# Attention on one core: scores by rows, P turned by DMA and V as the stationary operand in every second unit

## The chip, the cores and the metric

The kernel runs on one core of a Trainium2 chip. The metric is the device time in microseconds (us). All runs used here are in the fast state, except one single run (turn4) whose state is unknown; executions of one kernel mostly agree within 0.3%. PE is TensorE's matmul row in the traces and PEld its weight loads; ACT is ScalarE, DVE VectorE, POOL GpSimd, and SP is SyncE, whose queue issues the transposes. The *landing* of a transfer is the time from its issue until all its data has arrived. A ratio is the mean time of one kernel's runs over that of the other's of the same rounds, so it is not quite the ratio of the medians that are quoted.

## The reference, cut to what matters

```python
h = _layernorm(x) * (1 + ca) + sa                      # x: 2048 x 512
q = h @ wq                                             # 32 query heads of 128
k, v = repeat(k_cache, 4), repeat(v_cache, 4)          # 8 key/value heads, 2048 keys
scores = q @ k.T * 128 ** (-0.5)
p = softmax(scores)
o = p @ v
x = x + ga * (o @ wo)                                  # 4096 -> 512
# ... then a gated MLP with a 2048 x 2048 spatial matmul
```

## The kernel before

A *unit* is one of the 8 key/value heads with one tile of 128 queries: four query heads, 512 (head, query) columns, 2048 keys. There are 128 units. The loop runs one iteration per unit, in eight slots. In each slot PE computes the scores of unit `it` and the product P times V of the unit before.

Scores are computed *by columns*: keys on the partitions, (head, query) along the columns. The exponential writes P in just that layout, which P times V needs: contraction over keys, so keys on partitions. P is the stationary operand (the weight), and a column of ones beside V gives the sums of the softmax for nothing but one column.

```python
def qk(u, i):                       # slot i of unit u
    s_ps = bank2()                  # one of two score buffers, 128 x 1024
    for h in range(2):
        kt = 2 * i + h
        nc.tensor.matmul(s_ps[:, h * 512 : (h + 1) * 512],
                         lhsT=kT[:, kt * P : (kt + 1) * P],
                         rhs=qTs[b][:, :, jj * P : (jj + 1) * P])
    nc.scalar.activation(out=pTs[u][:, 2 * i : 2 * i + 2, :], in_=s_ps, func=ACT.Exp, ...)

def pv(u, i):                       # 64 matmuls of 129 columns per unit
    ...
        nc.tensor.matmul(o_ps[:, hh % 2, 0 : DH + 1],
                         lhsT=pTs[u][:, kt, hh * P : (hh + 1) * P],   # P: the weight
                         rhs=v1[:, kt, 0 : DH + 1])                   # V and the ones
    ...                             # reciprocal of the sums, multiplication, then:
    nc.sync.dma_start_transpose(out=oTs[u], in_=onorms[u])            # 128 KB

for it in range(NU + 6):
    for i in range(8):
        qk(it, i); pv(it - 1, i)
        ...                         # query projection (slots 0-3), output projection (4-7)
```

Cuts are marked by dots; tile shapes and flags are left out.

## Time and profile before

| | before |
|---|---|
| time, median (range) of the three runs before the prediction | 1321.16 us (1320.73 to 1321.49) |
| PE busy, and share of the chain | 99%, 99% |
| weight loads (PEld) | 65% of the span, beside the matmuls |
| ACT, DVE busy | 82%, 36% |
| transposing and plain DMA issued by SP (queue 1) | 37.65 MB |

"Busy" says little of PE, whose matmuls overlap. The column to read is the last one of a group, the idle time before it, and beside it the spacing from start to start. The lines are in the prediction.

### The profile page before, as it was taken

To read this page: it belongs to the slowest core of one execution; us is meant where nothing else is said; L and a number is where in the kernel's file an instruction comes from. 1 tells how busy PE (TensorE), PEld (TensorE's weight loads), DVE (VectorE), ACT (ScalarE), POOL (GpSimd) and SP (SyncE) were. 2 spreads that over 40 slices of the span, in tenths; PEclk is the share of its full clock that TensorE was granted. 3 is DMA by queue.
4 is the path that set the end of the run, shared out by engine and by line. 5 is a ranking of instruction groups with operands and counts; after the bars stand their busy time and mean duration, and the time that the engine had idled before them with its cause. 6 is when DMAs were issued, how large, how long until landed. Compare 5 with 4: busy or idle time off the path is not lost.

```text
span 1319.7 us, 27930 instructions
## 1 busy us (share of the span) xinstructions
PE 1312.4 (99%) x12359; PEld 858.6 (65%) x12359; DVE 470.7 (36%) x1162; ACT 1077.1 (82%) x1061; POOL 51.4 (4%) x96
## 2 busy tenths in 40 slices
PE   9999999999999999999999999999999999999998
PEld 5666666666666666666666666666666666644445
DVE  5622222222222222222222222222222566794444
ACT  7899999999999999999999999999999999650000
POOL 1201000000000000000000000000000000020000
PEclk9999999999999999999999999999999999999999
DMA  6542121112101111211110211121111112144300
GB/s 180 146 99 46 21 45 37 37 17 50 37 17 37 30 37 37 33 33 38 33 38 13 53 38 33 17 53 22 33 13 21 25 31 32 34 114 81 70 20 26
DMA packets 148944, 58.64 MB, mean 44 GB/s; under 512 B 138480, under 2 KB 144880, under 8 KB 148816
## 3 DMA queue, kind: packets, MB, share of 16 engines
q1 hardware_dynamic: 141792, 37.65, 15.4%
q0 software_dynamic: 4432, 16.91, 4.5%
q10 hardware_dynamic: 2592, 2.23, 0.5%
q8 instruction: 98, 1.61, 0.5%
q14 instruction: 30, 0.25, 0.1%
HBM read 21.89 MB, written 2.10 MB: 18 GB/s over the span
## 4 chain that ended last, share of the span: by engine, by line
PE 99%; DVE 0%; ACT 0%; issue 0%; DVEq 0%
PE o_ps L995 35%; PE s_ps L973 33%; PE misc L1027 8%; PE misc L940 8%; PE misc L1336 7%; PE s_ps L1182 2%; PE s_ps L1221 2%; PE o_ps L1357 1%; PE o_ps L781 1%; PE s_ps L1357 1%; PE misc L850 0%; DVE hT L809 0%; PE misc L1344 0%; ACT pT L980 0%; DVE tmp L1369 0%; DVE yout L1370 0%
## 5 line engine op out<-in xcount | busy, mean ns | idle before, releaser
L980 ACT ACTIVATE pT<-s_ps 128x1024 bf16<-128x1024 f32 x1024 | 1043.8, 1024 | 82.0 <-PE s_ps L973 6.7
L995 PEld LDWEIGHTS <-pT 128*128 128x128 bf16 x8192 | 548.5, 98 | 241.2
L995 PE MATMUL o_ps<-v,pT 128*128 128x129 bf16 x8192 | 631.5, 220 | 0.0
L973 PE MATMUL s_ps<-qT,kT 128*128 128x512 bf16 x2048 | 608.9, 379 | 0.3 <-ACT pT L980 0.2
L1006 DVE RECIPROCAL rall<-o_ps 128x2 f32<-128x2 f32 x256 | 43.5, 170 | 744.5 <-PE o_ps L995 741.1
L973 PEld LDWEIGHTS <-kT 128*128 128x128 bf16 x2048 | 199.3, 98 | 119.2 <-issue 0.8
L1027 PE MATMUL misc<-wo_g,oT 128*128 128x512 bf16 x512 | 194.1, 379 | 0.0
L940 PE MATMUL misc<-hT,wq_g 128*128 128x512 bf16 (+2 forms) x528 | 190.7, 371 | 0.1
L1007 DVE TENSOR_TENSOR onorm<-o_ps,rall 128x256 bf16<-128x256 f32 x256 | 108.6, 424 | 8.8
L1336 PE MATMUL misc<-wsp,z 128*128 128x512 bf16 (+2 forms) x560 | 100.7, 336 | 0.0
L951 DVE CAST qT<-misc 128x512 bf16<-128x512 f32 x127 | 86.2, 679 | 2.0 <-PE misc L940 2.0
L1336 PEld LDWEIGHTS <-z 128*128 128x128 bf16 x560 | 50.6, 98 | 48.5
L1040 DVE TENSOR_TENSOR xacc<-misc,xacc 128x512 f32<-128x512 f32 x112 | 76.0, 678 | 0.0
L940 PEld LDWEIGHTS <-wq_g 128*128 128x128 bf16 x528 | 50.4, 98 | 1.2 <-issue 0.4
L1027 PEld LDWEIGHTS <-oT 128*128 128x128 bf16 x512 | 50.1, 98 | 0.8
L1351 DVE TENSOR_TENSOR gb<-misc,bsp_bc 128x512 bf16<-128x512 f32 (+1 forms) x28 | 18.4, 658 | 58.9 <-PE misc L1336 58.9
L1182 PE MATMUL s_ps<-win_sb,hT 128*128 128x448 bf16 x128 | 27.0, 352 | 0.0
L1192 ACT ACTIVATE z<-s_ps 128x896 bf16<-128x896 f32 x16 | 14.7, 917 | 14.9 <-PE s_ps L1182 14.9
L1221 PE MATMUL s_ps<-hT,win_sb 128*128 128x512 bf16 x112 | 24.5, 379 | 0.0
L1229 ACT ACTIVATE z1T<-s_ps 128x1024 bf16<-128x1024 f32 x14 | 14.3, 1023 | 10.1 <-PE s_ps L1221 9.1
L692 DVE BATCH_NORM_STATS2 bnst<-x_sb 128x6 f32<-128x512 bf16 x32 | 21.8, 683 | 1.3 <-DMA x_sb<-in_A_x_dram 0.8
L1357 PE MATMUL o_ps<-wout_sb,yT 128*128 128x512 bf16 x84 | 20.1, 379 | 0.0
(88 smaller groups left out, 269.6 us busy)
## 6 DMA issues: line engine op xcount, KB each, us to landing
wq_g<-in_A_wq_dram POOLq DMA_DIRECT2D x7, 512.0 KB, 3.8
v<-in_A_v_cache_dram POOLq DMA_DIRECT2D x7, 512.0 KB, 6.0
wo_g<-in_A_wo_dram POOLq DMA_DIRECT2D x7, 512.0 KB, 4.7
oT<-onorm SPq DMA_TRANSPOSE x128, 2.4
wsp<-in_w_mod_dram POOLq DMA_DIRECT2D x1, 2048.0 KB, 9.0
out_dram<-yout ACTq DMA_DIRECT2D x16, 128.0 KB, 1.7
win_sb<-in_B_w_in_dram POOLq DMA_DIRECT2D x1, 1792.0 KB, 7.8
x_sb<-in_A_x_dram SPq DMA_DIRECT2D x3, 512.0 KB, 5.6
```

What stands on the lines that cost most here:

```text
L940: nc.tensor.matmul(ps[0][:, o0 : o0 + n], lhsT=wqs[g][:, dt, hh * DH : (hh + 1) * DH], rhs=hTs[ch][:, dt, c0 : c0 + n], start=(dt == 0), s ...
L951: nc.vector.tensor_copy(out=dst, in_=src)
L973: nc.tensor.matmul(s_ps[:, h * 512 : (h + 1) * 512].rearrange("p (r q) -> p r q", r=REP), lhsT=groups[g]["kT"][:, kt * P : (kt + 1) * P], ...
L980: nc.scalar.activation(out=pTs[u][:, 2 * i : 2 * i + 2, :], in_=s_ps[:].rearrange("p (k q) -> p k q", k=2), func=ACT.Exp, scale=inv_sqrt_dh,)
L995: nc.tensor.matmul(o_ps[:, hh % 2, 0 : DH + 1], lhsT=pTs[u][:, kt, hh * P : (hh + 1) * P], rhs=groups[g]["v1"][:, kt, 0 : DH + 1], start=( ...
L1007: nc.vector.tensor_tensor(out=onorms[u][:, hh - 1 : hh + 1, :], in0=o_ps[:, :, 0:DH], in1=rall[:, c0 : c0 + 2].unsqueeze(2).to_broadcast([ ...
L1027: nc.tensor.matmul(X_ps[:], lhsT=oTs[u][:, hh, :], rhs=groups[g]["wo"][:, hh, :], start=(hh == 0), stop=(hh == REP - 1),)
L1040: nc.vector.tensor_tensor(out=xaccs[j][:], in0=X_ps[:], in1=xaccs[j][:], op=ALU.add)
L1182: nc.tensor.matmul(ps[0][:, hf * 512 : hf * 512 + FC], lhsT=h2Ts[j // CT][:, dt, (j % CT) * P : (j % CT + 1) * P], rhs=win_sb[:, dt, FH + ...
L1221: nc.tensor.matmul(ps[0][:, k * 512 : (k + 1) * 512], lhsT=win_sb[:, dt, f * P : (f + 1) * P], rhs=h2Ts[2 * ch2 + k][:, dt, :], start=(dt ...
L1336: nc.tensor.matmul(g_ps[:, :n], lhsT=z2[:, st, f * P : (f + 1) * P], rhs=wsp[t][:, st, c0 : c0 + n], start=(st == 0), stop=(st == NT - 1 a ...
L1357: nc.tensor.matmul(dst, lhsT=yT[:, f, jj * P : (jj + 1) * P], rhs=wout_sb[:, f, :], start=(f == 0), stop=(f == NFT - 1),)
```

## The change

Its apparent intent is to cut the number of P times V matmuls and weight loads by four. With V as the weight, one load serves all four heads, and 512 columns of P stream past it: 16 matmuls of 512 columns in place of 64 of 129. The ones column is gone then (V fills all 128 weight columns), so the sums must come from elsewhere. In the changed units the scores are computed *by rows* (queries on partitions), where ACT can sum along the row while it exponentiates. But then P lies the wrong way round, and DMA has to turn it: four transposes of 512 KB per unit. Every second unit does it (even units 12 to 110, 50 in all; all units would probably be too much, since with half of them the DMA engines are already busy 73 to 89% in mid-attention, but no run tried it), and its P times V runs three iterations later instead of one.

```diff
+    TURN_A, TURN_B = 3 * CT, (HKV - 1) * NT            # 12, 112
+    def by_rows(u):
+        return TURN_A <= u < TURN_B and u % 2 == 0
+    def pv_at(u):
+        return u + 3 if by_rows(u) else u + 1
@@ qk
+        if by_rows(u):
+            hh, half = divmod(i, 2)
+            for c in range(2):
+                ...  matmul(s_ps[...], lhsT=qTs[b][:, hh, ...], rhs=kT[:, k0 : k0 + 512])
+            nc.scalar.activation(out=pn[hh][...], in_=s_ps[:], func=ACT.Exp,
+                                 scale=inv_sqrt_dh, accum_out=rsums[u][:, i : i + 1])
+            if half == 1:
+                at(*divmod(u * NSLOT + i + 2, NSLOT), lambda: turn_rows(u, hh))
+    def turn_rows(u, hh):            # sums added, reciprocal, P scaled in place, then
+        ...
+        nc.sync.dma_start_transpose(out=pTs[u][:, :, hh * P : (hh + 1) * P], in_=pn[hh])
+    def pv_rows(u, i, n):
+        for kt in range(i * NKT // n, (i + 1) * NKT // n):
+            nc.tensor.matmul(o_pss[u][:], lhsT=groups[g]["v1"][:, kt, 0:DH],
+                             rhs=pTs[u][:, kt, :], ...)
+        if i == n - 1:
+            nc.vector.tensor_copy(out=oTs[u][:], in_=o_pss[u][:]...)
@@ buffers and loads
+    pn = three slices of win_sb and one of wmod_a      # free at that time
+    odd units keep P in the buffer "wsp"
+    win_sb and the first spatial weights are loaded after unit 114
+    query projection of block 4 moves to iteration 13, which has no P times V
```

(Iteration 113 gets two P times V products.)

More of the change, by code (lines that the diff above doesn't have):

```diff
@@ L655 @@
     mhalf = res.tile([P, CT], FP32, name="mhalf")
-    win_sb = res.tile([P, NDT, F], BF16, name="win_sb")
+    win_t = res.tile([P, NDT * F], BF16, name="win_sb")
+    win_sb = win_t[:].rearrange("p (k f) -> p k f", k=NDT)
     wmod_a = res.tile([P, NDT, 2 * D], BF16, name="wmod_a")
+    pn = [win_t[:, r * SK : (r + 1) * SK] for r in range(REP - 1)]
+    pn.append(wmod_a[:].rearrange("p k n -> p (k n)")[:, 0:SK])
     wmod_b = wspp.tile([P, NDT * 4 * D], BF16, name="wsp")[:].rearrange(
@@ L926, with qproj @@
     warm(2)
-    def qproj(b, heads, c0, n):
+    def qproj(b, heads, c0, n, banks=("misc", "misc")):
         g, ch = divmod(b, NCH)
@@ L937, in mm @@
             if dt == 0 and (not one or hh == heads[0]):
-                ps[0] = bank("misc")
+                ps[0] = bank(banks[hh % 2])
             o0 = (hh - heads[0]) * n if one else 0
@@ L958 @@
     NU = HKV * NT
-    pTs, onorms, oTs, xaccs, o_pss, h2Ts = {}, {}, {}, {}, {}, {}
+    TURN_A, TURN_B = 3 * CT, (HKV - 1) * NT
[3 more added lines that the diff above has]
+        return u + 3 if by_rows(u) else u + 1
+    rsums, pTs, onorms, oTs, xaccs, o_pss, h2Ts = {}, {}, {}, {}, {}, {}, {}
     later = {}
@@ L968, in qk @@
         if i == 0:
-            pTs[u] = late.tile([P, NKT, 512], BF16, name="pT")
-        s_ps = bank2()
+            if TURN_A <= u <= TURN_B + 1 and u % 2 == 1:
+                pTs[u] = wspp.tile([P, NT, 512], BF16, name="wsp")
+            else:
+                pTs[u] = late.tile([P, NKT, 512], BF16, name="pT")
+            if by_rows(u):
+                rsums[u] = stat.tile([P, NSLOT], FP32, name="rs")
+        s_ps = bank2()
+        if by_rows(u):
+            hh, half = divmod(i, 2)
+            for c in range(2):
+                k0 = (2 * half + c) * 512
+                nc.tensor.matmul(
+                    s_ps[:, c * 512 : (c + 1) * 512],
+                    lhsT=qTs[b][:, hh, jj * P : (jj + 1) * P],
+                    rhs=groups[g]["kT"][:, k0 : k0 + 512],
+                    start=True,
+                    stop=True,
+                )
+            nc.scalar.activation(
+                out=pn[hh][:, half * HK : (half + 1) * HK],
+                in_=s_ps[:],
+                func=ACT.Exp,
+                scale=inv_sqrt_dh,
+                accum_out=rsums[u][:, i : i + 1],
+            )
+            if half == 1:
+                at(*divmod(u * NSLOT + i + 2, NSLOT), lambda: turn_rows(u, hh))
+            return
         for h in range(2):
@@ L985, in qk @@
         )
+    def turn_rows(u, hh):
+        c0 = u * REP + hh
+        rs, rinv = rsums[u], rall[:, c0 : c0 + 1]
+        tot = stat.tile([P, 1], FP32, name="tot")
+        nc.vector.tensor_tensor(
+            out=tot[:], in0=rs[:, 2 * hh : 2 * hh + 1], in1=rs[:, 2 * hh + 1 : 2 * hh + 2], op=ALU.add
+        )
+        nc.vector.reciprocal(out=rinv, in_=tot[:])
+        nc.vector.tensor_scalar(
+            out=pn[hh], in0=pn[hh], scalar1=rinv, scalar2=None, op0=ALU.mult
+        )
+        nc.sync.dma_start_transpose(
+            out=pTs[u][:, :, hh * P : (hh + 1) * P], in_=pn[hh]
+        )
+    def pv_rows(u, i, n):
+        g = u // NT
+        if i == 0:
+            o_pss[u] = bank("o_ps")
+        for kt in range(i * NKT // n, (i + 1) * NKT // n):
+            nc.tensor.matmul(
+                o_pss[u][:],
+                lhsT=groups[g]["v1"][:, kt, 0:DH],
+                rhs=pTs[u][:, kt, :],
+                start=(kt == 0),
+                stop=(kt == NKT - 1),
+            )
+        if i == n - 1:
+            oTs[u] = late.tile([P, REP, P], BF16, name="oT", bufs=3)
+            nc.vector.tensor_copy(
+                out=oTs[u][:], in_=o_pss[u][:].rearrange("p (r q) -> p r q", r=REP)
+            )
     def pv(u, i):
@@ L1144 @@
     at(2, 5, lambda: nc.gpsimd.dma_start(out=wmod_b, in_=wmod_dram[:, :, 2 * D : NMOD]))
-    at(5, 5, lambda: nc.gpsimd.dma_start(out=win_sb[:], in_=win_dram))
+    at(TURN_B + 3, 5, lambda: nc.gpsimd.dma_start(out=win_sb, in_=win_dram))
     at(9, 4, mod_cols_b)
@@ L1149, in set_fill @@
     def set_fill(b):
-        fs = qproj(b, list(range(REP)), 0, 512)
+        hole = TURN_A + 1 if (TURN_A + 1) // CT == b - 1 else None
+        fs = qproj(b, list(range(REP)), 0, 512, ("misc", "o_ps" if hole else "misc"))
         for k, fn in enumerate(fs):
             it, slot = (b - 1) * CT + k // NDT, k % NDT
+            if hole:
+                it, slot = hole, k // 2
             if b == 1:
@@ L1161, in wsp0 @@
         wsp[0] = wspp.tile([P, NT, 512], BF16, name="wsp")
-    at(20, 0, wsp0)
+    at(TURN_B + 4, 0, wsp0)
     for st in range(NT):
-        at(21 + 6 * st, 2, lambda st=st: load_wsp(wsp[0], 0, st))
+        at(TURN_B + 4 + st // 2, 2 + 4 * (st % 2), lambda st=st: load_wsp(wsp[0], 0, st))
     for g in range(1, HKV):
@@ L1257, with pv_part @@
         at(NU + 5, 5 + ch, lambda ch=ch: z2_norm(ch))
+    def pv_part(u, i, n):
+        if by_rows(u):
+            return pv_rows(u, i, n)
+        for k in range(NSLOT // n):
+            pv(u, i * (NSLOT // n) + k)
     for it in range(NU + 6):
@@ L1266 @@
             zs["z2"] = z2p.tile([P, NT, FH], BF16, name="z2")
-        wf = wo_proj(it - 3) if 3 <= it < NU + 3 else []
+        pvs = [u for u in (it - 3, it - 1) if 0 <= u < NU and pv_at(u) == it]
+        wos = [u for u in (it - 5, it - 3) if 0 <= u < NU and pv_at(u) + 2 == it]
+        wf = [fn for u in wos for fn in wo_proj(u)]
         for i in range(NSLOT):
@@ L1272 @@
                 qk(it, i)
-            if 1 <= it <= NU:
-                pv(it - 1, i)
+            if len(pvs) == 1:
+                pv_part(pvs[0], i, NSLOT)
+            elif pvs:
+                n = NSLOT // 2
+                pv_part(pvs[i // n], i % n, n)
             for fn in fill.pop((it, i), []):
                 fn()
-            if i >= 4 and wf:
-                wf[i - 4]()
+            if i >= NSLOT - len(wf):
+                wf[i - NSLOT + len(wf)]()
             if it >= NU:
                 zrun(3)
-        if 3 <= it < NU + 3 and it - 3 >= (HKV - 1) * NT:
-            ln2(it, (it - 3) % NT)
+        for u in wos:
+            if u >= (HKV - 1) * NT:
+                ln2(it, u % NT)
         if it == NU + 2:
```

## The prediction

> **What bounds the kernel now.** I read the page first (busy shares, the chain that ended last), then the costliest groups, then the order of time inside one slot of the attention loop, then ACT where it runs without waiting, then the DMA issues.
>
> ```profile
> span 1319.7 us, 27930 instructions
> ...
> PE 1312.4 (99%) x12359; PEld 858.6 (65%) x12359; DVE 470.7 (36%) x1162; ACT 1077.1 (82%) x1061; POOL 51.4 (4%) x96
> ...
> PE 99%; DVE 0%; ACT 0%; issue 0%; DVEq 0%
> ...
> L980 ACT ACTIVATE pT<-s_ps 128x1024 bf16<-128x1024 f32 x1024 | 1043.8, 1024 | 82.0 <-PE s_ps L973 6.7
> ...
> L995 PE MATMUL o_ps<-v,pT 128*128 128x129 bf16 x8192 | 631.5, 220 | 0.0
> L973 PE MATMUL s_ps<-qT,kT 128*128 128x512 bf16 x2048 | 608.9, 379 | 0.3 <-ACT pT L980 0.2
> L1006 DVE RECIPROCAL rall<-o_ps 128x2 f32<-128x2 f32 x256 | 43.5, 170 | 744.5 <-PE o_ps L995 741.1
> ```
>
> The chain is PE from end to end, and neither the scores (L973) nor P times V (L995) ever waits: 0.3 and 0.0 us of idle time before them. So time is the sum of PE's start-to-start spacings. A mean duration (220, 379 ns) is not the spacing, because matmuls overlap; the order of time gives it:
>
> ```profile
> 480.93 0.59 PE L973 MATMUL s_ps<-qT,kT 128*128 128x512 bf16 x2
> 481.36 0.62 PE L995 MATMUL o_ps<-v,pT 128*128 128x129 bf16 x8
> 481.82 0.38 PE L940 MATMUL misc<-hT,wq_g 128*128 128x512 bf16 x1
> 482.03 0.59 PE L973 MATMUL s_ps<-qT,kT 128*128 128x512 bf16 x2
> ```
>
> This is one slot, 1.10 us: two score matmuls of 512 columns, eight P times V matmuls of 129, one other of 512. From the starts in the trace between 250 and 1000 us, a matmul of 512 columns takes 215.85 ns to the next start and one of 129 columns 56.65 ns. A unit is eight slots: 16 x 215.85 + 64 x 56.65 + 8 x 215.85 = 3.45 + 3.63 + 1.73 = 8.81 us, which is the spacing of the turned-output transfers in the DMA queue (1.24 + 7.57).
>
> ACT does one exponential of 1024 columns per slot. Where PE has run ahead it goes back to back:
>
> ```profile
> 1128.69 4.69 ACT L980 ACTIVATE pT<-s_ps 128x1024 bf16<-128x1024 f32 x5
> ```
>
> The first four start-to-start spacings here are 0.90 us (4.69 less the last duration of 1.06, over four, within 10 ns). So ACT can do a slot in 0.90 and is paced by PE at 1.10: 0.20 us per slot in hand, and no more.
>
> **What the Trainium skill says.** "TensorE: Matmul & The Clock Gate", section "Back-to-back issue gap", gives about 81 ns per matmul of 128 columns in a stream of load-and-multiply pairs, and 56 ns for the bare gap. This trace has 56.65 ns with a new weight load for every one of them, so here the loads (98 ns each, beside the matmuls) cost nothing and the smaller figure holds. That decides what the change can win. "ScalarE: Activation LUTs", section "What ACT_TABLE_LOAD costs": an ACTIVATE with immediate scale takes 186 ns + 0.833 ns per column, and consecutive ones overlap by about 93 ns. For 1024 columns that is 1039 and a spacing of 946; the trace has 1.02 and 0.90, close and a little better. I found no page that prices ACT's sum output; "VectorE: DVE Perf Modes", section "Two Vector instructions with no wait between them", says that on Vector an op with accumulator output is two instructions. "DMA: Bandwidth & Descriptors", section "Latency and other measured facts", has 261 GB/s for a transposing DMA with a broken-up middle dimension; the trace has less:
>
> ```profile
> 498.26 1.83 SPq L739 DMA_TRANSPOSE kT<-in_A_k_cache_dram  x1
> ...
> 532.25 1.19 SPq L1015 DMA_TRANSPOSE oT<-onorm  x1
> ```
>
> The first moves 512 KB and is done with its packets about 2.6 us after the first of them, the second 128 KB in 0.66 us: both near 200 GB/s. The queue is held 1.83 us for the large one (1.36 in other groups) and 1.19 us for the small one.
>
> **The change, part by part.** By rows are the even units from 12 to 110: 50 units.
>
> *PE.* Scores: the same 16 matmuls of 512 columns, operands swapped. P times V: 64 matmuls of 129 columns (3.626 us) become 16 of 512 (3.454 us). That is 64 x 129 = 8256 columns against 8192, and 48 fewer starts at roughly 2.5 to 3 ns (56.65 ns less 129/2.4). Gain 0.172 us per unit, x 50 = 8.6 us. The 48 weight loads that go were hidden already. The two shapes alternate: P times V of a row unit runs three iterations later, beside the scores of an odd unit, so each iteration has still one P times V.
>
> *The hole.* Iteration 13 has no P times V and iteration 113 has two. Query projections are moved into 13, which leaves 12, 14 and 15 thin. PE sums: 12 and 14: 20 x 0.2158 + 3.63 = 7.94 us each; 13: 36 x 0.2158 = 7.77; 15: 32 x 0.2158 = 6.91; together 30.6. ACT in the same four: two column units at 8 x 0.90 = 7.2 and two row units at 8.4 to 9.2, together 31.2 to 32.8. PE idles here for about 1.5 us, once.
>
> *ACT.* Same 1024 columns per call, plus reading out the sum, in 8 x 50 = 400 calls. With the page's fixed 186 ns and overlap of 93, a one-column extra instruction adds between 0.09 (overlapped) and 0.19 (alone): an estimate of 1.0 to 1.1 us per call against a slot of 1.10. If it is more, ACT falls behind inside a row unit, but there are two score buffers: score matmuls i+2 must start 1.77 us after scores i end (two slots less 0.43), and the exponential needs 1.02 plus a hand-over of say 0.07, so ACT may lag by about 0.68 us before PE stops. The next unit pays it back at (1.08 - 0.90) x 8 = 1.4 us. So PE sees nothing until 8 x (call - 1.10) exceeds 0.68, a call of 1.19 us.
>
> *DVE.* Removed per row unit: two reciprocals (170 ns) and two multiplications (424), 1.2 us. Added: four times an add and a reciprocal (about 170 each) and a scaling of 2048 columns. Scalings with two pointers took 306, 404 and 504 ns at 128, 512 and 896 columns, 0.26 ns per column, so some 0.8 us; with the copy of the output (679, as the other 512-column copies) 5.2 us. Per pair of units DVE goes from 5.1 to 9.1 us of 17.4. All off the chain: each PSUM bank that it frees has four slots of time.
>
> *DMA.* One 128 KB transpose per row unit goes, four of 512 KB come: at 200 GB/s 2.6 us each, 10.5 us per pair, 11.2 with the one left, of 17.4 us, or 64% of the engines. The last is issued one slot into the next unit and read at the start of the third: about 14 us for an issue of 1.4 to 1.8 and 2.6 of transfer. The other loads (projection weight, moved spatial weights) keep to stages with room.
>
> Sum: 1321.2 - 8.6 + 1.5 = 1314 us.
>
> **Rivals.**
> 1. *ACT becomes the bound in row units.* For it: only 0.20 us in hand per call, and nothing in this trace shows what the sum costs. Against: the lag allowance. A call of 1.23 us means 8 x 0.13 - 0.68 = 0.36 us of stall per row unit, 18 us in all, 1332 us. A call of 1.27 gives 0.68 x 50 = 34: 1348. I give 25% to any visible stall and about 8% to one beyond 1.27.
> 2. *The DMA queue's issue time.* If issuing grew with bytes from the small SBUF transposes (4 x 1.19 = 4.8 us), four plus one small are 20.3 us in a pair of 17.4: +2.9 x 50, about 1459 us. For it: both the small one and the new ones read SBUF, the cheap large one reads DRAM. Against: the 512 KB one held the queue 1.36 to 1.83 us only. 6%.
> 3. *Fewer weight loads free PE.* If the 98 ns loads cost PE something, 48 fewer per unit would win more. Against: 56.65 ns is shorter than one load, so they overlap wholly. 2%.
> 4. *All is hidden and nothing is won.* The transposes share SBUF with PE's reads, or small waits at the iteration borders eat 8.6 us: 1318 to 1323.
>
> **Range and chances.** The certain part of the gain is 0.65%, so faster by over 2% needs rival 3. The low end allows full gain, no hole and a little from the removed waits: 1306. The high end is rival 1 at a call of about 1.24: 1338. Slower by over 2% (over 1347.6) is the far part of rival 1 and rival 2: 13%.
>
> **What would show it.** Page of the changed kernel: PE still 99% of the chain; P times V split into 4992 matmuls of 129 columns and 800 of 512; the latter spaced 215.8 ns; row-unit iterations 8.81 us and odd ones 8.63. ACT's exponentials with sum spaced no more than 1.10 us when they pair with a row unit; idle time before L973's successors near 0 outside iterations 12 to 15. The new transposes hold the queue under 2 us and land within 5; DMA share some 60 to 70% in the middle; DVE about 44% busy. Wrong if the score matmuls of row units wait on ACT (rival 1), if the V-weighted matmuls wait on the transposes or the DMA queue never idles (rival 2), or if the iterations are not shorter although nothing waits (rival 4).

## The result, and the profile after

The changed kernel takes 1316.16 us (1315.49 to 1317.03, 4 runs) against 1321.06 us, ratio 0.9963 (95% interval 0.9946 to 0.9980): the same at 2%, faster by 0.37%. The prediction had 1314.0.

The page of the changed kernel, with the lines that answer to those of before; a group's columns are line, engine, operation, output and inputs, shapes and count, then busy time and mean ns of one, then the idle time before them and what ended it:

```profile
span 1314.1 us, 25092 instructions
...
PE 1305.1 (99%) x9959; PEld 755.5 (57%) x9959; DVE 657.4 (50%) x1612; ACT 1105.0 (84%) x1461; POOL 52.0 (4%) x96
...
PE 98%; DMA 1%; DVE 0%; issue 0%; ACT 0%; ACTq 0%; DVEq 0%
...
L1013 PE MATMUL s_ps<-qT,kT 128*128 128x512 bf16 x1248 | 370.9, 379 | 1.9 <-ACT wmod_a L1001 1.6
L1001 ACT ACTIVATE win_sb<-s_ps 128x1024 bf16<-128x1024 f32 x300 | 307.0, 1025 | 6.2 <-ACT win_sb L1001 0.8
...
L1069 PE MATMUL o_ps<-v,wsp 128*128 128x129 bf16 x3264 | 251.6, 220 | 0.0
L994 PE MATMUL s_ps<-kT,qT 128*128 128x512 bf16 x800 | 237.9, 379 | 0.0
L1048 PE MATMUL o_ps<-pT,v 128*128 128x512 bf16 x800 | 237.3, 379 | 0.0
...
L1035 DVE TENSOR_SCALAR win_sb<-win_sb,rall 128x2048 bf16<-128x2048 bf16 x150 | 113.0, 753 | 5.7 <-DVE rall L1034 0.5
...
L1001 ACT ACTIVATE wmod_a<-s_ps 128x1024 bf16<-128x1024 f32 x100 | 102.4, 1024 | 2.3 <-DMA pT<-wmod_a 2.3
```

There are 2400 fewer matmuls, and PE is the chain as before. The row scores (L994) and both kinds of P times V (L1048, L1069) wait for nothing. New is a small idle time before the column scores (L1013, 1.9 us where there were 0.3), ended by ACT; and in the last line ACT itself waits 2.3 us for a transposing DMA. The chain has 1% of DMA for the same reason.

One slot of an odd iteration, in which the P times V of a row unit runs (order of time, PE; start us, duration):

```profile
489.25 0.59 PE L1013 MATMUL s_ps<-qT,kT 128*128 128x512 bf16 x2
489.68 0.59 PE L1048 MATMUL o_ps<-pT,v 128*128 128x512 bf16 x2
490.11 0.38 PE L944 MATMUL misc<-hT,wq_g 128*128 128x512 bf16 x1
490.32 0.38 PE L1013 MATMUL s_ps<-qT,kT 128*128 128x512 bf16 x1
```

Slot to slot it is 1.07 to 1.08 us, where the kernel before had 1.10. Over a pair of iterations, from one output copy of a row unit to the next, the median is 17.44 us; two units of before take 2 x 8.81 = 17.62.

Busy time in a stretch of 150 us in mid-attention, before and then after. The columns are PE, weight loads, DVE, ACT and GpSimd in us (with counts), the granted clock, the DMA engines' share and GB/s:

```profile
850.00:1000.00 150.00, 150.00 (x1501) 101.74 (x1500) 40.48 (x102) 139.45 (x137) 2.13 (x3) 1.00 0.15 29
```

```profile
850.00:1000.00 150.00, 150.00 (x1115) 85.59 (x1114) 70.22 (x174) 145.42 (x202) 2.87 (x4) 1.00 0.73 144
```

Everything but PE has more to do: DVE 70 us for 40, the DMA engines 73% for 15%. PE is still full, and only the 0.17 us per row unit come out at the end.

**Where the time went.** For every matmul I took the time to the next start and subtracted the steady spacing of its shape; what remains is PE not working at its pace. The sums, in us:

| stretch | before | after |
|---|---|---|
| start to 110 us | 6.84 | 6.58 |
| 110 to 150 us (iterations 12 to 15) | 0.00 | 1.13 |
| 150 to 1000 us | 0.06 | 1.77 |
| 1000 to 1140 us (two products in one iteration) | 0.23 | 0.55 |
| 1140 us to the end | 1.78 | 1.78 |
| total | 8.92 | 11.80 |

The shape gives 50 x 0.172 = 8.6 us, and 2.9 are lost again: -5.7 us, against spans of 1319.7 and 1314.1 (-5.6). The 1.77 us of the third stretch are one single stop, at 541 us. ACT in order of time there, with the idle time and what ended it in brackets:

```profile
539.88 0.19 ACT L1001 ACTIVATION_READ_ACCUMULATOR win_sb<-s_ps 128x1 f32 x1
542.18 1.02 ACT L1001 ACTIVATE wmod_a<-s_ps 128x1024 bf16<-128x1024 f32 x1 [2.11 <-DMA pT<-wmod_a]
```

ACT may not overwrite the fourth head's rows (`wmod_a`) until the transpose of the unit before has read them. That one, from the DMA queue of SP, and what GpSimd issued then:

```profile
528.82 2.60 SPq L1038 DMA_TRANSPOSE pT<-wmod_a  x1
```

```profile
528.90 0.75 POOL L720 DMA_DIRECT2D wq_g<-in_A_wq_dram  x1 [64.68 <-PE misc L944]
```

A 512 KB weight load went out on GpSimd's own queue 0.08 us after the transpose. The transpose landed after 13.3 us (the median of all is 4.6), the load after 12.2 (3.8 in the kernel before). In mid-attention ACT comes back to the fourth head's buffer 11.0 us (median) after its transpose was issued; PE reads the turned rows only after 13.0. The load waits for the last query projection of an earlier group, which ends in slot 3 of an odd iteration, just where the fourth head's transpose starts: the schedule brings the two together in every group of 16 units.

### The profile page after: what moved, and what is told of

It reads as the page before. It is cut to its first block, busy times and chain, and to the rows that moved or that the text cites. A ratio compares the mean times of both kernels' runs of the same rounds, so it can differ in the third digit from the quotient of the medians.

```text
span 1314.1 us, 25092 instructions
## 1 busy us (share of the span) xinstructions
PE 1305.1 (99%) x9959; PEld 755.5 (57%) x9959; DVE 657.4 (50%) x1612; ACT 1105.0 (84%) x1461; POOL 52.0 (4%) x96
## 4 chain that ended last, share of the span: by engine, by line
PE 98%; DMA 1%; DVE 0%; issue 0%; ACT 0%; ACTq 0%; DVEq 0%
PE o_ps L1069 21%; PE s_ps L1013 20%; PE o_ps L1048 13%; PE s_ps L994 13%; PE misc L1101 8%; PE misc L944 8%; PE misc L1426 7%; PE s_ps L1260 2%; PE s_ps L1299 2%; PE o_ps L1447 1%; DMA pT<-wmod_a 1%; PE o_ps L785 1%; PE s_ps L1447 1%; PE misc L854 0%; PE o_ps L944 0%; DVE hT L813 0%
## 5 line engine op out<-in xcount | busy, mean ns | idle before, releaser
L1020 ACT ACTIVATE wsp<-s_ps 128x1024 bf16<-128x1024 f32 x408 | 416.2, 1025 | 19.5 <-PE s_ps L1013 3.5
L1013 PE MATMUL s_ps<-qT,kT 128*128 128x512 bf16 x1248 | 370.9, 379 | 1.9 <-ACT wmod_a L1001 1.6
L1001 ACT ACTIVATE win_sb<-s_ps 128x1024 bf16<-128x1024 f32 x300 | 307.0, 1025 | 6.2 <-ACT win_sb L1001 0.8
L1069 PEld LDWEIGHTS <-wsp 128*128 128x128 bf16 x3264 | 218.5, 98 | 96.3
L1069 PE MATMUL o_ps<-v,wsp 128*128 128x129 bf16 x3264 | 251.6, 220 | 0.0
L994 PE MATMUL s_ps<-kT,qT 128*128 128x512 bf16 x800 | 237.9, 379 | 0.0
L1048 PE MATMUL o_ps<-pT,v 128*128 128x512 bf16 x800 | 237.3, 379 | 0.0
L1020 ACT ACTIVATE pT<-s_ps 128x1024 bf16<-128x1024 f32 x216 | 217.3, 1026 | 20.6 <-PE s_ps L1013 8.3
L1013 PEld LDWEIGHTS <-kT 128*128 128x128 bf16 x1248 | 121.0, 98 | 117.0 <-issue 4.4
L1069 PEld LDWEIGHTS <-pT 128*128 128x128 bf16 x1728 | 115.3, 98 | 49.6
L1048 PEld LDWEIGHTS <-v 128*128 128x128 bf16 x800 | 78.2, 98 | 94.4
L1069 PE MATMUL o_ps<-v,pT 128*128 128x129 bf16 x1728 | 132.5, 220 | 0.0
L994 PEld LDWEIGHTS <-qT 128*128 128x128 bf16 x800 | 78.2, 98 | 52.5 <-issue 0.2
L1001 ACT ACTIVATE wmod_a<-s_ps 128x1024 bf16<-128x1024 f32 x100 | 102.4, 1024 | 2.3 <-DMA pT<-wmod_a 2.3
```

Of the source, the lines that this page charges most:

```text
L994: nc.tensor.matmul(s_ps[:, c * 512 : (c + 1) * 512], lhsT=qTs[b][:, hh, jj * P : (jj + 1) * P], rhs=groups[g]["kT"][:, k0 : k0 + 512], sta ...
L1001: nc.scalar.activation(out=pn[hh][:, half * HK : (half + 1) * HK], in_=s_ps[:], func=ACT.Exp, scale=inv_sqrt_dh, accum_out=rsums[u][:, i : ...
L1013: nc.tensor.matmul(s_ps[:, h * 512 : (h + 1) * 512].rearrange("p (r q) -> p r q", r=REP), lhsT=groups[g]["kT"][:, kt * P : (kt + 1) * P], ...
L1048: nc.tensor.matmul(o_pss[u][:], lhsT=groups[g]["v1"][:, kt, 0:DH], rhs=pTs[u][:, kt, :], start=(kt == 0), stop=(kt == NKT - 1),)
L1069: nc.tensor.matmul(o_ps[:, hh % 2, 0 : DH + 1], lhsT=pTs[u][:, kt, hh * P : (hh + 1) * P], rhs=groups[g]["v1"][:, kt, 0 : DH + 1], start=( ...
```

## The experiments

**Theory.** The gain is the shape of P times V on PE alone, 0.172 us per row unit, mostly fewer starts (a start here is one matmul with its weight load, beyond its columns). Sums, scaling and turning are hidden; what was lost is the hole at iteration 12 and the stop behind the weight load. **Rivals.** (a) The sums on ACT cost time in every row unit. (b) The gain is the dropped ones column, not the starts. (c) The transposes cost PE time without a visible wait. (d) The stop is nearly full DMA engines, not the meeting of two queues. Twelve kernels were run; all passed the comparison with the reference, those with a constant for the sums too, since here all of P is near 1/2048. The traces of vw50, vw_all, rows54, turn4 and the four kernels with extra ACT work lack a few per cent of the matmul records, so for those I read pair lengths and not gaps.

### after_again: the changed kernel once more

No edit.

> The changed kernel unaltered, as the yardstick of this series. Both theories: 1316 us. What it tells beside that: whether the one stop of PE of 1.8 us at 541 us in the first profile (score matmuls behind ACT, ACT behind the transposing DMA of the fourth head that was issued in the same tenth of a microsecond as a 512 KB weight load) comes back in another execution. If it belongs to the schedule it stands at the same place; if it is chance it is gone or elsewhere, and the runs of one kernel spread by some 1.5 us.

Measured: 1315.01 us (1314.64 to 1319.15, 5 runs), ratio 0.9963. Its profiled execution (1314.64 us) has no stop: 0.0 us of lost PE time between 150 and 1000 us, and 10.52 us in all. Without the stop the kernel is within 0.7 us of the predicted 1314.0. So whether PE stops in a given execution is chance, at a place that the schedule offers again and again; over nine executions the kernel spreads by 4.5 us, the kernel before by 0.8.

### wq_sync: the weight loads behind the transposes in one queue

```diff
-        at(it + 7, 3, lambda g=g: load_wq(g, nc.gpsimd))
+        at(it + 7, 3, lambda g=g: load_wq(g, nc.sync))
```

> Only the weight loads of the query projection move from GpSimd's queue to the SP queue, behind the fourth head's transpose. If the stop of 1.8 us comes from those loads running on a second queue beside the transposes, it goes and the time falls by 1 to 2 us to about 1314.5, with no PE gap over 0.5 us between 160 and 1000 us. If the stop is only the DMA engines being nearly full, the same bytes on one queue keep it: 1316.

Measured: 1314.28 us (1313.80 to 1314.30, 5 runs), ratio 0.9946. The stop is gone (0.0 us lost between 150 and 1000 us), and the spread falls from 4.5 to 0.5 us. The 95% intervals of the two ratios overlap, so the spread and the traces carry this, not the means. The SP queue in order of time:

```profile
215.16 2.03 SPq L1038 DMA_TRANSPOSE pT<-wmod_a  x1
217.25 0.94 SPq L720 DMA_DIRECT2D wq_g<-in_A_wq_dram  x1
218.24 3.70 SPq L743 DMA_TRANSPOSE kT<-in_A_k_cache_dram  x1
```

Rival (d) falls: in the 14 us after such a transpose the DMA engines move 179 to 206 GB/s at a busy share of 0.93 to 1.04 (four places), which is no idle stretch (113 GB/s at 1.17 around the stop, 528 to 542 us), and still no turned head after 130 us whose landing is recorded takes over 7 us.

But the edit changes two things at once. The load shares the queue, and it is issued 1.8 to 2.1 us behind the transpose, some 12 iterations later than on GpSimd's queue, which issued it as soon as its buffer was free. Which of the two helps, the one queue or the distance, is not separated.

The other profiles of this series support that the meeting matters: in v64 and in nosum, which keep GpSimd's loads, PE stopped for 1.6 and 1.4 us, each time behind a fourth head's transpose issued within 0.2 us of such a load and landing after 13.2 and 13.0 us. The four traces have 20 meetings of a load with a fourth head's transpose within 0.8 us. In the six where the transpose was issued 0.03 to 0.2 us before the load, it landed after 8.7 to 13.3 us; in the other 14 (later than the load, or more than 0.3 us before it) after 5.7 to 7.7. Three of the six stopped PE. So two queues alone do not make a transpose late; it goes by tenths of a microsecond, which differ from execution to execution; what the engines do in that case, the traces do not tell. That the slow unprofiled executions (1319.15 us) had more than one stop is likely and not shown.

### v64: V as the weight, but loaded again for each head

```diff
-        for kt in range(i * NKT // n, (i + 1) * NKT // n):
-            matmul(o_pss[u][:], lhsT=v1[:, kt, 0:DH], rhs=pTs[u][:, kt, :])
+        for m in range(i * REP * NKT // n, (i + 1) * REP * NKT // n):
+            hh, kt = divmod(m, NKT)
+            matmul(o_pss[u][:, hh * P : (hh + 1) * P], lhsT=v1[:, kt, 0:DH],
+                   rhs=pTs[u][:, kt, hh * P : (hh + 1) * P])
```

> V stays the weight, but each weight load is repeated for every head: 64 matmuls of 128 columns per row unit instead of 16 of 512; everything else is as in the changed kernel. Theory (the gain is 48 fewer starts at about 3 ns and 64 fewer columns): 64 x 56.3 = 3.60 us against 3.45, so +0.149 us x 50 = +7.5 us, about 1323.5, slower than the kernel before. Rival (the gain is the 64 columns of sums alone, 0.027 us per unit, and starts are free): +0 us, 1316.

Measured: 1322.08 us (1320.09 to 1324.93), ratio 1.0013: 7.1 us above the changed kernel, and the gain is gone. The pair takes 17.56 us against 17.44. So 48 starts cost 0.12 us, 2.5 ns each; that makes 55.8 ns for a matmul of 128 columns, not the 56.3 of the expectation, and 50 x 0.12 = 6 us of the 7.1; the stop in its profile is part of the rest. Rival (b) falls: of the 0.172 us per unit, 0.12 are starts and 0.05 are left for the ones column. v64 has all the weight loads back, and their 98 ns stay hidden. From its page between 250 and 1000 us:

```profile
L1049 PE MATMUL o_ps<-pT,v 128*128 128x128 bf16 x2725 | 207.8, 219 | 0.0
L1049 PEld LDWEIGHTS <-v 128*128 128x128 bf16 x2722 | 180.6, 98 | 80.2
```

But every matmul here has a load of its own, so v64 adds 48 loads and 48 matmuls together. Whether the 2.5 ns belong to the start of the matmul or to the change of weight, no run separates.

### nosum: ACT does not sum

```diff
                 scale=inv_sqrt_dh,
-                accum_out=rsums[u][:, i : i + 1],
@@
-                rsums[u] = stat.tile([P, NSLOT], FP32, name="rs")
+                rsums[u] = rs_const          # filled with 1024.0 once
```

> ACT no longer sums in the row units; a constant stands for the sums (results only near the reference, since all P are close to 1/2048). 400 reads of 0.19 us leave ACT, 78 us of its time. Theory (they fit in the slot, ACT is not on the chain outside the four thin iterations): row-unit exponentials go back to where PE paces them, time falls by 0.5 to 1.2 us, all of it between 117 and 150 us: 1315. Rival (the sums cost time in every row unit): falls by 4 us or more.

Measured: 1315.65 us (1314.27 to 1318.09), ratio 0.9959: no different from the changed kernel (1315.01). Unit 12, in the thin iterations, takes 7.94 us instead of 8.21; the pairs stay at 17.44. Rival (a) falls. The expected saving of about 1 us cannot be told from the scatter of the stops.

### vw50: V as the weight alone

```diff
# on the kernel before, in the same 50 units
+        if v_weights(u):
+            for kt in (2 * i, 2 * i + 1):
+                matmul(o_pss[u][:], lhsT=v1[:, kt, 0:DH], rhs=pTs[u][:, kt, :])
+            # last slot: oT = o_ps * (1 / 2048), instead of the sums
```

> One part alone, on the kernel before: in the same 50 units V is the weight of P times V, but scores stay by columns, P is not turned, ACT sums nothing, and the output is scaled by a constant 1/2048 in place of the sums (results only near the reference). No hole, no large transposes. Theory: -0.172 us x 50 = -8.6 us, and -0.0 elsewhere: 1312.5. The difference to the changed kernel, about 3.5 us, is then the price of the rest (hole, end, the one stop). Rival (the turned transposes take bandwidth from PE or the swapped score operands cost something): well under 1312.

Measured: 1313.02 us (1312.30 to 1313.17), ratio 0.9936: -8.15 us, where 8.6 were expected. The pair is 17.44 us, the same as with all the turning and summing. Rival (c) falls with it: 144 GB/s of DMA traffic, mostly transposes, do not change PE's spacing. The price of the rest is 1314.28 - 1313.02 = 1.3 us with the repaired load, and 2 to 3 us without.

### vw_all: the same in 116 units

```diff
# on vw50
-        return 3 * CT <= u < (HKV - 1) * NT and u % 2 == 0
+        return u >= 3 * CT
```

> V as the weight in every unit from 12 on (116 units), scores by columns, a constant in place of the sums, nothing turned: what the shape alone is worth. Theory: 116 x 0.172 = 20.0 us less than 1321.1, about 1301, if DVE and ACT stay off the chain (ACT 0.90 against a slot of 1.08). Rival (at a slot of 1.08 ACT, or the weight loads of V, begin to hold PE): less than 2.3 times the gain of the 50 units.

Measured: 1302.25 us (1301.84 to 1303.28), ratio 0.9859: -19.0 us, 2.3 times the gain of the 50 units, and the unit is 8.633 us long. The shape is worth the same in every unit. (By the core's span, 1299.7 us at the median against 1319.4, it is 19.7 us, close to the 20.0 reckoned; the rest lies outside the span.) But this kernel has no true sums, so it is a bound and not a version.

### act_half and act_full: more work on ACT in row units

```diff
                 accum_out=rsums[u][:, i : i + 1],
             )
+            if i % 2 == 1:                   # act_half; act_full: always
+                nc.scalar.activation(out=idle[:, 0:8], in_=ident[:, 0:8], func=ACT.Exp, ...)
```

> The changed kernel with an idle 8-column exponential after every second summed exponential: 200 more instructions on ACT. Theory (ACT may lag 0.68 us in a row unit before PE stops, and the next unit pays it back): four extra operations of 0.1 to 0.2 us are 0.4 to 0.8 us of lag, so 0 to 0.1 us per unit: 1316 to 1322. Rival (ACT at 1.10 us per call is already the pace of row units): +0.4 to 0.8 us x 50, 1336 to 1356.

> The same after every summed exponential: 400 more instructions. Theory: eight extra operations of 0.1 to 0.2 us are 0.8 to 1.6 us of lag less the allowance of 0.68: 0.1 to 0.9 us x 50 = 5 to 46 us, 1322 to 1362, and score matmuls of the row units wait on ACT. From both runs together the allowance can be read: stall per unit should be 8 x extra - 0.68 here and 4 x extra - 0.68 (or nothing) in the other. Rival: twice the loss of the other run.

Measured: 1318.08 us (1317.59 to 1318.30) and 1317.88 us (1316.12 to 1319.39), both ratio 0.9976. The pair is 17.44 us in both. The cost is the 2 to 3 us that the first turned units lose (unit 14 takes 11.8 and 10.9 us in place of 8.3 to 9.1; ACT waits there up to 2.4 us for transposes). It turned out that these runs could not test the lag allowance. Where ACT is limited, in unit 12 of after_again, the order of time shows

```profile
118.86 1.02 ACT L1001 ACTIVATE win_sb<-s_ps 128x1024 bf16<-128x1024 f32 x1
119.76 0.20 ACT L1001 ACTIVATION_READ_ACCUMULATOR win_sb<-s_ps 128x1 f32 x1
119.86 1.02 ACT L1001 ACTIVATE win_sb<-s_ps 128x1024 bf16<-128x1024 f32 x1
```

A summed call takes 1.00 us and not 1.10: the read of the sum is recorded with 0.20 us, but the next exponential starts 0.10 after it. The extra exponential of 8 columns added 0.095 us, so even act_full had calls of 1.10 us, just the slot. Two more kernels go further.

### act_128 and act_3x8: past the slot

```diff
# on wq_sync
+            nc.scalar.activation(out=idle[:], in_=ident[:], func=ACT.Exp, ...)        # act_128
+            for _ in range(3):                                                        # act_3x8
+                nc.scalar.activation(out=idle[:, 0:8], in_=ident[:, 0:8], func=ACT.Exp, ...)
```

> The repaired kernel with an idle exponential of 128 columns after every summed one. In the two earlier runs a summed call took 1.00 us where ACT was limited and 0.095 more with the 8-column one, so neither reached the slot of 1.10 us and they could not tell the lag allowance. Here a call should take 1.00 + 0.095 + 0.10 = 1.19 to 1.20. Allowance theory: 8 x 0.10 - 0.68 = 0.1 us per unit, +2 to 8 us, 1316 to 1322, row-unit pairs of 17.44 to 17.55 us. Rival (no allowance, every call over 1.10 is paid): 0.8 us x 50 = +40 us, 1354, pairs of 18.2.

> The repaired kernel with three idle 8-column exponentials after every summed one: a call of 1.00 + 3 x 0.095 = 1.28 us. Allowance theory: 8 x 0.18 - 0.68 = 0.76 us per unit, +38 us and a few in the thin iterations, about 1354, pairs of 18.2, and the score matmuls of the second half of a row unit wait on ACT. No allowance: +72 us, 1386, pairs of 18.9. Averaging over the pair without limit (ACT pays back all in the next unit): 8 x 1.28 + 8 x 0.90 = 17.5, nearly nothing.

Measured: 1333.70 us (1333.6 to 1333.9) and 1485.59 us (1485.3 to 1486.3), ratios 1.0094 and 1.1245.

| | summed call, us | pair, us | over 17.44 | 8 x (call - 1.10) | allowance |
|---|---|---|---|---|---|
| act_full | 1.10 | 17.44 | 0 | 0 | - |
| act_128 | 1.196 | 17.80 | 0.36 | 0.76 | 0.40 |
| act_3x8 | 1.58 | 20.82 | 3.38 | 3.83 | 0.45 |

act_3x8 missed its expected call (1.28): the three idle operations, which write the same tile, took 0.58 us together and not 0.29. Both rows still give the same allowance, 0.40 to 0.45 us. So ACT can lag in a row unit and pay it back in the next one, as the theory says, but by less than the 0.68 us reckoned with; why, no run shows. The bound on a summed call is thus 1.10 + 0.43 / 8 = 1.15 us. The real one of 1.00 is 0.15 away from it.

### turn4: the same bytes in four times as many transposes

```diff
-        dma_start_transpose(out=pTs[u][:, :, hh * P : (hh + 1) * P], in_=pn[hh])
+        for q in range(4):
+            dma_start_transpose(out=pTs[u][:, 4 * q : 4 * q + 4, hh * P : (hh + 1) * P],
+                                in_=pn[hh][:, q * 512 : (q + 1) * 512])
```

> Each transpose of 128x2048 is cut into four of 128x512, the same bytes. Theory (issuing costs the queue 1.2 us per transpose whatever its size between 128 and 512 KB): 17 issues in a pair of units, 17 x 1.24 = 21.1 us against 17.4, so the SP queue becomes the bound: +3.6 us x 50 = +180 us, about 1495, with the P times V of row units waiting on DMA. Rival (issue time grows with bytes, so cutting changes nothing): 1316.

Measured: 1619.0 us (one run, state unknown; the mean granted clock was 0.947, where the other runs have 0.997 to 1.000, so a part of the loss may be the clock's). The pair is 23.3 us. From the order of time of SP's queue and from the list of waits (who waited for what: us in total, times, longest):

```profile
502.74 15.61 SPq L1039 DMA_TRANSPOSE pT<-win_sb  x12
518.45 1.21 SPq L1091 DMA_TRANSPOSE oT<-onorm  x1
519.76 6.02 SPq L1039 DMA_TRANSPOSE pT<-wmod_a  x4
```

```profile
PE misc L1103 <- DMA oT<-onorm: 163.9, 51, 6.3
```

The queue hardly rests (it is held 94% of the time between 300 and 900 us): twelve issues in 15.61 us are 1.30 us each, 17 make 22.1, with their waits the 23.3 of the pair. The expectation had 21.1 and +180 us; it is +303. The direction and the queue were right, the place of the wait was not. PE waits not at the row units' P times V but at the output projection of the odd units, whose small transpose stands in the same queue. That the changed kernel issues 512 KB at a time is therefore a condition of its working at all.

### rows54: the version that beats both

```diff
# on wq_sync
-    TURN_A, TURN_B = 3 * CT, (HKV - 1) * NT
+    TURN_A, TURN_B = 3 * CT, (HKV - 1) * NT + NT // 2
```

> The repaired kernel (projection weights loaded on the SP queue) with four more row units, up to unit 118 in place of 110, and the loads that wait for their buffers moved by eight iterations. Theory: 4 x 0.172 = 0.7 us less than 1314.3, about 1313.6, as long as the moved loads still land in time. Rival (the later loads of the last stage come late, or the two P times V in one iteration now fall among the second normalisation): 1315 or more.

Measured: 1313.42 us (1313.15 to 1313.68, 6 runs), ratio 0.9940, correct: 0.9 us below wq_sync, where 0.7 were expected. The difference between these two is across two series whose runs of the kernel before differ by 0.15 us. Against the changed kernel it is 1.6 to 2.7 us, without its spread.

## Why the prediction was right, and where not

The time was in the range, 2.2 us above the centre.

- **PE's gain, 8.6 us: right.** 17.44 us per pair, as 8.81 + 8.63; vw50 alone gave 8.15, and vw_all 19.0 for 116 units (20.0 reckoned). Its division was a little off: a start costs 2.5 ns (v64), the lower end of "roughly 2.5 to 3". The 2.4 columns per ns in its working come out of the spacings too: (512 - 129) / (215.85 - 56.65) is 2.41, and 2.40 with the 55.8 ns of v64.
- **The hole, 1.5 us: right in kind,** 1.13 us in iterations 12 to 15 (1.79 in after_again) and another 0.3 where two products share an iteration.
- **ACT's sums, 0.09 to 0.19 us: right at the lower end,** 0.09 to 0.10 where ACT is limited. The lag allowance of 0.68 us was mis-sized: 0.40 to 0.45 by act_128 and act_3x8. It decided nothing, because the call stayed under the slot; that is luck in part, since with a call between 1.15 and 1.19 us PE would have stopped where the prediction saw nothing. Rival 1 did not come true.
- **DVE: right** to 0.05 us per operation (scaling 0.753 us for 0.8, add 0.154 for 0.17, output copy 0.691 for 0.679). The page shows 50% busy, where 44% had been said; that was a slip, since the prediction's own sum (470.7 us and 50 times 4.0 more) is 51% of the span.
- **DMA: bytes and landing right, load too low.** The turned heads land after a median of 4.6 us (within 5 was said), but the share in mid-attention was 73 to 89%, not 60 to 70%, and the queue is held 1.8 to 2.3 us at the median, not under 2. The trace before could have warned: its seven 512 KB transposes held the queue 1.36 to 2.74 us, and the prediction quotes 1.36 and 1.83 alone. Rival 2 did not come true, though turn4 shows that it is real once the transposes are small.
- **The step that failed** is the last sentence on DMA: "The other loads (projection weight, moved spatial weights) keep to stages with room." The projection weight is released in the very slot in which the fourth head is turned. When the transpose goes out just before the load, the meeting costs 4 to 9 us of landing time, and at the far end that is more than the margin. The margin was taken from the wrong reader, too: "about 14 us" is until PE reads the turned rows (13.0 measured), but ACT overwrites the buffer they come from after 11.0, and it was ACT that waited. This is the stop of 1.8 us in the first profile and, with it, most of the 2.2 us that the prediction missed; wq_sync, with the loads put in line, comes to 1314.28.
- **Rivals 3 and 4** did not come true: v64 brings 48 loads per unit back and loses 2.5 ns on each, not 98, and vw50 with no transposes has the same pair length.

## What to carry to other kernels

When PE is full, count its columns and its matmuls, not the duration of its weight loads: here 48 fewer matmuls at 2.5 ns beyond their columns, and 64 fewer columns, are the whole gain, and everything that was moved to ACT, DVE and DMA for their sake only had to stay hidden. Before giving an engine more, compare its call with the slot that it serves and find how far it may lag; before giving a DMA queue more, look at what else is issued in the same slot, also on other queues. Times that scatter more than before (4.5 us here, against 0.8) can mean a wait that only sometimes lasts too long, and the profile of a single execution may show it or miss it.

## What the Trainium skill lacked or had wrong

- "ScalarE: Activation LUTs" has no price for the sum output of an ACTIVATE. These runs: 0.194 us in the record, and 0.09 to 0.10 us more from start to start where ACT is the limit (1.00 us against 0.90 for 1024 columns).
- "TensorE: Matmul & The Clock Gate", section "Back-to-back issue gap", gives about 81 ns for a 128-column matmul with its weight load in a sustained stream. Here it is 55.8 ns (v64) and 56.65 ns with 129 columns, a new weight for each. Its figure for 512 columns in the same sentence, about 131 ns, does not hold here either: 215.85 ns.
- "DMA: Bandwidth & Descriptors", section "Rules for kernel authors", says that a transpose next to ordinary DMAs "needs nothing". The row is about corruption, and the data did come out right; on time it is silent. In 6 of 20 meetings with a 512 KB load from GpSimd's queue the 512 KB transpose landed only after 8.7 to 13.3 us, where the median of all is 4.6; with the load on the same queue, about 2 us behind, none did. Nor does the page give an issue time for a transposing DMA by size that it says is this chip's: here the medians are 1.2 to 1.3 us for 128 KB and 1.8 to 2.3 for 512 KB.
